# Retention attention feeding a gated FFN on one core: an earlier place for the first weight loads, and the small tables built on other engines

## The chip, the core and the metric

The kernel runs on one core of a Trainium2 chip. A core has a matrix engine (TensorE, PE in the profile), a vector engine (VectorE, DVE), a scalar engine (ScalarE, ACT), GpSimd (POOL), a queue engine (SyncE, SP), and 16 DMA engines that move data between the main memory and the on-chip memory. The engines run side by side and wait for one another through semaphores. Each engine works through its own instructions in order. The metric is device time in microseconds; the time before is a median of 228.19 us over 8 runs.

## What is computed

Two stages follow each other. The first is a retention recurrence over 768 steps for 4 batches and 8 heads of width 64; the second is a feed-forward network with a sigmoid gate on the 3072 resulting rows of width 512 (inner width 1536):

```python
gamma = 1.0 - 2.0 ** (-5.0 - np.arange(H))          # one decay per head
for t in range(S):                                   # S = 768
    state = gamma * state + k[:, :, t] (outer) v[:, :, t]
    y[:, :, t] = scale * q[:, :, t] @ state
x = y.transpose(0, 2, 1, 3).reshape(B * S, H * D)    # 3072 x 512
gate = sigmoid(x @ w_gate); val = x @ w_val          # 512 x 1536 each
out = (gate * val) @ w_out                           # 1536 x 512
```

All inputs and the output are float32 in main memory; the matrix products are in bf16.

## The kernel before

The recurrence is cut into 6 tiles of 128 steps. Within a tile the sum over earlier steps is a masked 128x128 score matrix per head (with powers of gamma as the mask), and what lies in earlier tiles comes through a 64x64 state per head. The feed-forward part of one tile (512 rows: 4 batches of 128 steps) has 12 column groups of the gate and value products (`up_part`, L413) and then the output product (`down`, L449). The order of all instructions is written out by hand: the first tile line by line (L486 to L581), the later tiles by a list of group numbers (`plan`), in which attention of later tiles is put between matmul groups.

What matters here is the first tile, where everything starts at once:

- The first two batches' k come in float32 through SP and ACT (`kf`, L101 and L102) and are cast to bf16 in two halves, one by VectorE (L173), one by ScalarE (L174).
- All other loads of the first tile cast while they move, and are issued by GpSimd: q of batches 0 and 1, k and q of batches 2 and 3, v of batches 0 to 3 (L109 to L117, ten loads). Then come the first weights (`load_w`, L79): `wg` and `wv`, columns 0 to 255, each in two halves of 128 KB (as they land, in bf16), and then columns 256 to 511 and 512 to 767 with 256 KB a load (slabs 1 and 2). GpSimd's loads take turns on eight semaphores, so the ninth and every later load waits until the load eight places before it has landed.
- Tables. `ahead` and `after` (L110, L111) are index tables that GpSimd's iota makes. From `after` VectorE makes four exponents of the mask (`decay_power`, L152), which ScalarE takes through exp (`decay_exp`, L156). `ident` (L147), the identity for the transposes, comes from `ahead`. `lgz` (L146) holds the logarithms of the decays. `tok`, `begin` and `col` (L118 to L120) are three more iotas; from `col` and `lgz` GpSimd makes the exponents of `taby` (L189), from `tok` and `begin` VectorE makes those of `tabs` and `tabz` (`later_constants`), and ScalarE takes these three through exp (`later_exps`, L184 to L186). `taby` is first used by the second tile.
- TensorE: 11 dummy products on zeros (`keep_on`, L480; further ones fill later waits), transposes of k and q (`first_transpose`, L352), scores (L362), which VectorE masks (L369), the product with v (`first_y`, L379), copied into `xT` (L384), and then the first gate and value products (`first_part`, L422), first over k-tiles 0 and 1, then over 2 and 3, so that each half of the weights is used when it lands. After that follow the groups of L413.
- GpSimd's further work behind the slabs: `first_scaled` (L388, two products for each half), which wait for the exp of `tabs`, more weight loads, the tables of the later tiles.

Of the kernel before, what the change touches and what calls it, by code (L numbers as in the profile page):

```python
# [10 lines left out]
AX = mybir.ActivationFunctionType  # L11
ALU = mybir.AluOpType
# [3 lines left out]
def kernel(  # L16
# [12 lines left out]
    nc = tc.nc  # L29
    B, H, S, D = q.shape  # L30
    N_TOK, D_MODEL = out.shape
    D_FF = moe_w_gate.shape[1]
    C = 128
    NT = S // C
    NP = H // 2
# [37 lines left out]
    wg = wpool.tile([128, KT, D_FF], BF16, name="wg")  # L73
    wv = wpool.tile([128, KT, D_FF], BF16, name="wv")
    wo = wpool.tile([128, NFF, D_MODEL], BF16, name="wo")

    def load_w(dst, w, s, kk=slice(0, KT)):
        cols = slice(s * 256, (s + 1) * 256)
        nc.gpsimd.dma_start(out=dst[:, kk, cols], in_=w.rearrange("(kk p) n -> p kk n", p=128)[:, kk, cols])  # L79

    def load_gate_val(s):
        load_w(wg, moe_w_gate, s)
        load_w(wv, moe_w_val, s)
# [8 lines left out]
    def first(dst, x, b, eng):  # L92
        j = b % 2
        eng.dma_start(out=dst[j * D:(j + 1) * D].rearrange("p h r d -> p h (r d)"),  # L94
                      in_=x[b, :, 0:C, :].rearrange("h (p r) d -> p h (r d)", r=2))

    kf = ld.tile([C, H, 2, D], F32, tag="kf", name="kf", bufs=1)
    k2, q2, v2 = [[ld.tile([C, H, 2, D], BF16, tag=tag, name=tag, bufs=n) for _ in range(2)]
                  for tag, n in (("kn", 6), ("qn", 4), ("vs", 6))]
# [4 lines left out]
    ahead = const.tile([128, C], F32, name="ahead")  # L104
    after = const.tile([128, 3, D], F32, name="after")
    tok = const.tile([128, NT], F32, name="tok")
    begin = const.tile([128, NT], F32, name="begin")
    col = const.tile([128, C], F32, name="col")
    first(q2[0], q, 0, nc.gpsimd)  # L109
    nc.gpsimd.iota(ahead, pattern=[[-1, C]], base=0, channel_multiplier=1, allow_small_or_imprecise_dtypes=True)  # L110
    nc.gpsimd.iota(after, pattern=[[1, 3], [-2, D]], base=-1, channel_multiplier=2, allow_small_or_imprecise_dtypes=True)  # L111
    first(q2[0], q, 1, nc.gpsimd)
    for x, t in ((k, k2[1]), (q, q2[1])):
        for b in (2, 3):
            first(t, x, b, nc.gpsimd)
    for b in range(4):
        first(v2[b // 2], v, b, nc.gpsimd)  # L117
    nc.gpsimd.iota(tok, pattern=[[C, NT]], base=0, channel_multiplier=1, allow_small_or_imprecise_dtypes=True)  # L118
    nc.gpsimd.iota(begin, pattern=[[C, NT]], base=0, channel_multiplier=0, allow_small_or_imprecise_dtypes=True)
    nc.gpsimd.iota(col, pattern=[[1, C]], base=0, channel_multiplier=0, allow_small_or_imprecise_dtypes=True)  # L120

# [3 lines left out]
    nlg = const.tile([128, 2, NP], F32, name="nlg")  # L127
    lgz = const.tile([128, 2, NP], F32, name="lgz")
    lsc = const.tile([128, 1], F32, name="lsc")
    ident = const.tile([128, 128], BF16, name="ident")  # L130
# [5 lines left out]
    taby = const.tile([128, NP, C], F32, name="taby")  # L136
# [3 lines left out]
    nc.vector.memset(lsc, math.log(scale))  # L140
    for h in range(H):
        nc.vector.memset(nlg[:, h % 2, h // 2:h // 2 + 1], -lg[h])
    for e in range(2):
        hd = slice(e * D, (e + 1) * D)
        for j in range(2):
            nc.vector.tensor_scalar(lgz[hd, j], nlg[hd, e ^ j], -1.0, None, op0=ALU.mult)  # L146
    nc.vector.tensor_scalar(ident, ahead, 0.0, None, op0=ALU.is_equal)  # L147
    nc.vector.tensor_scalar(after[D:128], after[D:128], -2.0 * D, None, op0=ALU.add)
    since = after.rearrange("s r p -> s (r p)")

    def decay_power(g, e):
        nc.vector.tensor_tensor(decay[:, g, e], since.unsqueeze(1).to_broadcast([128, 2, 3 * D]),  # L152
                                nlg[:, e, 2 * g:2 * g + 2].unsqueeze(2).to_broadcast([128, 2, 3 * D]), op=ALU.mult)

    def decay_exp(g, e):
        nc.scalar.activation(decay[:, g, e], decay[:, g, e], AX.Exp, bias=lsc)  # L156
# [3 lines left out]
    def tab_power(x, lo, n):  # L160
        nc.vector.tensor_tensor(tabs_of[:, :, :, lo:lo + n], x.unsqueeze(1).unsqueeze(1).to_broadcast([128, NP, 2, n]),
                                nlg.rearrange("s e p -> s p e").unsqueeze(3).to_broadcast([128, NP, 2, n]), op=ALU.mult)
# [1 line left out]
    tab_power(after[:, 1:3, 0], NT, 2)  # L164
    nc.vector.scalar_tensor_tensor(since, since, -1.0e6, since, op0=ALU.mult, op1=ALU.min)
    kb = k2[0]
    decay_power(0, 0)
    decay_power(0, 1)
    decay_power(1, 0)
    decay_exp(0, 0)  # L170
    decay_exp(0, 1)
    decay_exp(1, 0)
    nc.vector.tensor_copy(kb[:, 0:4], kf[:, 0:4])  # L173
    nc.scalar.copy(kb[:, 4:8], kf[:, 4:8])  # L174
    decay_power(1, 1)

    def later_constants():
        tab_power(tok, 0, NT)
        shape = [128, NT, 2, NP]
        nc.vector.tensor_tensor(tabz, lgz.unsqueeze(1).to_broadcast(shape),  # L180
                                begin.unsqueeze(2).unsqueeze(3).to_broadcast(shape), op=ALU.mult)

    def later_exps():
        nc.scalar.activation(taby, taby, AX.Exp, bias=lsc)  # L184
        nc.scalar.activation(tabs, tabs, AX.Exp)
        nc.scalar.activation(tabz[:, 1:], tabz[:, 1:], AX.Exp)  # L186

    def taby_power():
        nc.gpsimd.tensor_tensor(taby, col.unsqueeze(1).to_broadcast([128, NP, C]),  # L189
                                lgz[:, 0].unsqueeze(2).to_broadcast([128, NP, C]), op=ALU.mult)  # L190

    taby_power()
    for dst, w in ((wg, moe_w_gate), (wv, moe_w_val)):
        load_w(dst, w, 0, slice(0, 2))
        load_w(dst, w, 0, slice(2, 4))
    load_gate_val(1)
    load_gate_val(2)

    def last_constants():
        nc.vector.tensor_scalar(causal, ahead, 0.0, None, op0=ALU.is_le)  # L200
# [15 lines left out]
    def bank(shape, dt=F32):  # L216
        return pf.tile(shape, dt, tag="ff", name="ff")

    def half(e):
        return slice(e * D, (e + 1) * D)  # L220
# [126 lines left out]
    def first_transpose(i, which, g, eng):  # L347
        tp = bank([128, 2, 2, C], BF16)
        for p in range(2):
            for r in range(2):  # L350
                for e in range(2):
                    nc.tensor.transpose(tp[half(e), p, r ^ which], (k2, q2)[which][i][:, 4 * g + 2 * p + e, r, :], ident)  # L352
        eng(kq2[i][:, which, 2 * g:2 * g + 2], tp)

    def first_scores(i, g):
        t = kq2[i]
        s = [bank([128, 2, 2, C]) for _ in range(2)]
        for p in range(2):
            for r in range(2):
                for j in range(2):  # L360
                    for e in range(2):
                        nc.tensor.matmul(s[e][half(j), p, r].rearrange("s (o p) -> s o p", o=2),  # L362
                                         t[half(e), 0, 2 * g + p, r, half(j)], t[half(e), 1, 2 * g + p, :, half(j)],
                                         start=True, stop=True)
        for e in range(2):
            st0[i, g, e] = at.tile([128, 2, 2, C], BF16, tag=f"st{e}", name=f"st{e}", bufs=4)
            d = decay[:, g, e]
            d = bass.AP(d.tensor, d.offset, [d.ap[0], d.ap[1], (D, 2), (1, C)])
            nc.vector.tensor_tensor(st0[i, g, e], s[e], d, op=ALU.mult)  # L369
# [107 lines left out]
    def keep_on(n):  # L477
        u = bank([128, 512])
        for _ in range(n):
            nc.tensor.matmul(u, zero[:, :128], zero, start=True, stop=True)  # L480
# [5 lines left out]
    keep_on(11)  # L486
    first_transpose(0, 0, 0, dve)
    first_transpose(0, 0, 1, act)
    decay_exp(1, 1)
    keep_on(1)  # L490
    first_transpose(0, 1, 0, dve)
    first_transpose(0, 1, 1, act)
    keep_on(1)
    first_scores(0, 0)
    first_scores(0, 1)
    later_constants()
    keep_on(1)
    first_transpose(1, 0, 0, act)
# [6 lines left out]
    first_y(0, (act, act))  # L505
    first_scores(1, 1)
    later_exps()
    keep_on(3)
    gate0 = first_part(wg, 0)
# [128 lines left out]
```

## Time and profile before

| What | Value |
|---|---|
| median of 8 runs | 228.19 us (227.27 to 230.99) |
| the profiled execution's own time | 230.57 us |
| its span in the profile | 228.8 us |
| TensorE busy | 218.8 us (96%) |
| VectorE / ScalarE / GpSimd busy | 111.3 / 69.9 / 105.9 us |
| bytes moved by DMA | 25.75 MB, mean 113 GB/s |
| granted TensorE clock over the span | 0.991 of full speed |

The profiled execution is one of the eight runs, and one of the longest. 1.77 us of its time lie outside the span. Times in the profile count from the start of the span. An operation's line gives its start, the time that it takes (for a group of several: from the first start to the last end), the engine, the source line, what it writes and reads, and, in brackets, how long the engine sat idle before it and what ended the wait. A DMA has two parts: the short instruction with which a queue issues it, and the transfer, which lands some us later. The GB/s and DMA rows count the bytes that the 16 DMA engines moved and how busy these were.

### The profile page before, as it was taken

Reading aid. Unit: us, or ns where it says so; the run is one execution under the profiler, and the core shown is the slowest. Engines: PE = TensorE matmul, PEld = TensorE weight load, DVE = VectorE, ACT = ScalarE, POOL = GpSimd, SP = SyncE. Lnnn points to the kernel's source line nnn. Section 1 sums busy time; section 2 is a strip of 40 time slices with the busy share of each in tenths; the row PEclk is TensorE's granted clock in tenths of the full one; section 3 lists DMA queues with packets and bytes.
Section 4 is the critical chain, followed back from the end, with each engine's and each line's share of the span. In section 5 each row is a group of like instructions: output and inputs, shape, how many; then the busy total and the mean of one; then the engine's idle time right before and its main releaser. Section 6 shows DMA issues by size and latency. Waiting matters only on the chain.

```text
span 228.8 us, 4913 instructions
## 1 busy us (share of the span) xinstructions
PE 218.8 (96%) x2037; PEld 118.2 (52%) x2061; DVE 111.3 (49%) x193; ACT 69.9 (31%) x117; POOL 105.9 (46%) x133
## 2 busy tenths in 40 slices
PE   7876999999999999999999999999999999999994
PEld 2545444547888655445445444545444444444443
DVE  6751384145784676944914634923544812343301
ACT  4654323432223211433311433211433311433221
POOL 7999697960994986719276073370000000000000
PEclk9997999999999999999999999999999999999999
DMA  7999999998999999999979879799500012100022
GB/s 125 177 146 168 196 146 169 185 146 179 138 131 126 190 154 197 148 106 90 125 93 161 172 52 117 75 133 141 133 6 0 3 46 95 46 1 0 3 92 92
DMA packets 99702, 25.75 MB, mean 113 GB/s; under 512 B 87648, under 2 KB 96736, under 8 KB 99680
## 3 DMA queue, kind: packets, MB, share of 16 engines
q0 software_dynamic: 75808, 13.90, 76.4%
q1 hardware_dynamic: 23200, 11.21, 23.4%
q10 hardware_dynamic: 672, 0.33, 0.5%
q8 instruction: 16, 0.26, 0.5%
q14 instruction: 6, 0.05, 0.1%
HBM read 28.31 MB, written 6.29 MB: 151 GB/s over the span
## 4 chain that ended last, share of the span: by engine, by line
PE 90%; POOL 5%; DMA 3%; issue 1%; DVE 0%; POOLq 0%
PE ff L413 53%; PE ff L449 26%; DMA wv<-in_moe_w_val_dram 3%; PE ff L284 2%; PE ff L261 2%; PE ff L422 2%; PE ff L277 2%; POOL qn L94 1%; PE ff L466 1%; PE ff L302 1%; POOL vs L94 1%; POOL wg L79 1%; POOL kn L94 1%; POOL taby L189 0%; PE ff L232 0%
## 5 line engine op out<-in xcount | busy, mean ns | idle before, releaser
L433 DVE TENSOR_TENSOR hT<-gs,ff 128x512 bf16<-128x512 f32 x72 | 49.0, 686 | 62.6 <-PE ff L413 57.8
L413 PE MATMUL ff<-xT,wg 128*128 128x512 bf16 (+1 forms) x323 | 71.5, 348 | 0.6 <-issue 0.2
L413 PE MATMUL ff<-xT,wv 128*128 128x512 bf16 (+1 forms) x324 | 71.0, 347 | 0.1
L432 ACT ACTIVATE gs<-ff 128x512 f32<-128x512 f32 x72 | 43.0, 597 | 85.6 <-PE ff L413 80.3
L449 PE MATMUL ff<-wo,hT 128*128 128x512 bf16 x263 | 60.9, 379 | 1.0 <-issue 0.5
L413 PEld LDWEIGHTS <-wv 128*128 128x128 bf16 x328 | 32.1, 98 | 28.4
L413 PEld LDWEIGHTS <-wg 128*128 128x128 bf16 x328 | 31.8, 98 | 28.2 <-issue 0.6
L449 PEld LDWEIGHTS <-hT 128*128 128x128 bf16 x276 | 26.3, 98 | 30.7
L453 ACT COPY ob<-ff 128x512 f32<-128x512 f32 x23 | 13.5, 586 | 58.4 <-PE ff L449 56.3
L267 DVE TENSOR_TENSOR st<-ff,maskk 128x512 bf16<-128x512 f32 x40 | 24.8, 682 | 6.4 <-PE ff L261 6.4
L295 DVE TENSOR_TENSOR xT<-ff,taby 128x512 bf16<-128x512 f32 x20 | 12.9, 686 | 30.3 <-PE ff L284 30.3
L548 POOL COPY held<-kqX 128x1 bf16<-128x1 bf16 x7 | 1.3, 184 | 39.9 <-DMA kqX<-qn 32.4
L243 POOL TENSOR_TENSOR ks<-kn,tabsk 128x1024 bf16<-128x1024 bf16 x8 | 16.0, 2001 | 0.5 <-PE ff L413 0.3
L67 POOL DMA_DIRECT2D qn<-in_q_dram x20 | 15.4, 802 | 0.0
L67 POOL DMA_DIRECT2D kn<-in_k_dram x20 | 15.2, 774 | 0.0
L57 POOL DMA_DIRECT2D vs<-in_v_dram x10 | 12.1, 1212 | 0.6 <-DMA kn<-in_k_dram 0.5
L63 POOL DMA_DIRECT2D kn<-in_k_dram x10 | 9.3, 929 | 1.8 <-issue 1.8
L63 POOL DMA_DIRECT2D qn<-in_q_dram x10 | 9.3, 926 | 0.0
L480 PE MATMUL ff<-zero 128*128 128x512 bf16 x19 | 7.6, 528 | 1.2 <-DVE zero L139 1.2
L315 DVE TENSOR_TENSOR zb<-za,tabz 128x512 bf16<-128x512 f32 x10 | 8.5, 857 | 0.2
L284 PE MATMUL ff<-st,vs 128*64 128x128 bf16 x160 | 6.4, 222 | 0.0
L261 PE MATMUL ff<-kqX 64*64 64x128 bf16 x288 | 5.6, 217 | 0.0
(80 smaller groups left out, 117.5 us busy)
## 6 DMA issues: line engine op xcount, KB each, us to landing
out_dram<-ob SPq DMA_DIRECT2D x19, 256.0 KB, 3.0
vs<-in_v_dram POOLq DMA_DIRECT2D x10, 256.0 KB, 7.5
qn<-in_q_dram POOLq DMA_DIRECT2D x14, 128.0 KB, 4.5
kn<-in_k_dram POOLq DMA_DIRECT2D x12, 128.0 KB, 4.3
wo<-in_moe_w_out_dram POOLq DMA_DIRECT2D x4, 384.0 KB, 6.9
wg<-in_moe_w_gate_dram POOLq DMA_DIRECT2D x5, 256.0 KB, 8.4
wv<-in_moe_w_val_dram POOLq DMA_DIRECT2D x5, 256.0 KB, 9.0
kn<-in_k_dram POOLq DMA_DIRECT2D x20, 64.0 KB, 4.4
```

The source lines that it names most:

```text
L57: nc.gpsimd.dma_start(out=vs[i], in_=v[2 * h:2 * h + 2, :, t * C:(t + 1) * C, :].rearrange("b h s d -> s (b h) d"))
L63: nc.gpsimd.dma_start(out=tiles[i][:, 0:H], in_=src[0])
L67: nc.gpsimd.dma_start(out=dst[:, e], in_=pairs[:, 1 - e])
L243: nc.gpsimd.tensor_tensor(ks[i], kn[i], tabsk[:, i // 2].rearrange("s j h -> s (j h)").unsqueeze(2) .to_broadcast([C, 2 * H, D]), op=ALU.mult)
L267: nc.vector.tensor_tensor(st[i, j], sc[i, j][e], maskk[:, e ^ j], op=ALU.mult)
L284: nc.tensor.matmul(y[i, j][half(e), p, :], vs[i][:, j * H + 2 * p + e, :], st[:, p, :], start=False, stop=True, skip_group_check=True)
L295: nc.vector.tensor_tensor(xT[t][:, :, c:c + C], y[i, j], taby, op=ALU.mult)
L413: nc.tensor.matmul(u[:, i * n:(i + 1) * n], w[:, kk, n1 * 128:(n1 + 1) * 128], xT[t][:, kk, lo:hi], start=(kk == 0), stop=(kk == KT - 1))
L432: nc.scalar.activation(g, ps[0], AX.Sigmoid)
L433: nc.vector.tensor_tensor(hT[t][:, n1s[0]:n1s[-1] + 1, lo:hi], g.rearrange("p (i n) -> p i n", n=n), ps[1].rearrange("p (i n) -> p i n", n ...
L449: nc.tensor.matmul(o, hT[t][:, n1, b * C:(b + 1) * C], wo[:, n1, :], start=(n1 == 0), stop=(n1 == NFF - 1))
L453: nc.scalar.copy(ob, o)
```

## The change

The weight loads of columns 0 to 767 are issued right behind the four loads of v. The iotas of `tok`, `begin` and `col` and the product for `taby`, which stood between them on GpSimd, are gone from it: VectorE now makes `begin` by six memsets, `col` from `ahead`, `taby`'s exponents behind `lgz`, and `tok` from `begin` and `ahead`. The iotas of `ahead` and `after` stand ahead of GpSimd's first load (q of batch 0) and not behind it. On VectorE, `ident` and `lgz` come after the four `decay_power`s, all four of which, and `col` and `taby`, stand ahead of its half of the cast of k. On ScalarE the fourth `decay_exp` stands with the other three, ahead of the cast of k, and the exp of `taby` moves from behind the first two copies into `xT` to a place behind the transposes of q of batches 0 and 1. TensorE's order is as it was.

```diff
-    first(q2[0], q, 0, nc.gpsimd)
     nc.gpsimd.iota(ahead, pattern=[[-1, C]], base=0, channel_multiplier=1, allow_small_or_imprecise_dtypes=True)
     nc.gpsimd.iota(after, pattern=[[1, 3], [-2, D]], base=-1, channel_multiplier=2, allow_small_or_imprecise_dtypes=True)
+    first(q2[0], q, 0, nc.gpsimd)
     first(q2[0], q, 1, nc.gpsimd)
...
     for b in range(4):
         first(v2[b // 2], v, b, nc.gpsimd)
-    nc.gpsimd.iota(tok, pattern=[[C, NT]], base=0, channel_multiplier=1, allow_small_or_imprecise_dtypes=True)
-    nc.gpsimd.iota(begin, pattern=[[C, NT]], base=0, channel_multiplier=0, allow_small_or_imprecise_dtypes=True)
-    nc.gpsimd.iota(col, pattern=[[1, C]], base=0, channel_multiplier=0, allow_small_or_imprecise_dtypes=True)
+    for dst, w in ((wg, moe_w_gate), (wv, moe_w_val)):
+        load_w(dst, w, 0, slice(0, 2))
+        load_w(dst, w, 0, slice(2, 4))
+    load_gate_val(1)
+    load_gate_val(2)
...
-    for e in range(2):
-        hd = slice(e * D, (e + 1) * D)
-        for j in range(2):
-            nc.vector.tensor_scalar(lgz[hd, j], nlg[hd, e ^ j], -1.0, None, op0=ALU.mult)
-    nc.vector.tensor_scalar(ident, ahead, 0.0, None, op0=ALU.is_equal)
+    for t in range(NT):
+        nc.vector.memset(begin[:, t:t + 1], float(t * C))
...
-    decay_power(0, 0)
-    decay_power(0, 1)
-    decay_power(1, 0)
-    decay_exp(0, 0)
-    decay_exp(0, 1)
-    decay_exp(1, 0)
+    for g in range(2):
+        for e in range(2):
+            decay_power(g, e)
+            decay_exp(g, e)
+    nc.vector.tensor_scalar(ident, ahead, 0.0, None, op0=ALU.is_equal)
+    for e in range(2):
+        hd = slice(e * D, (e + 1) * D)
+        for j in range(2):
+            nc.vector.tensor_scalar(lgz[hd, j], nlg[hd, e ^ j], -1.0, None, op0=ALU.mult)
+    nc.vector.tensor_scalar(col, ahead, ahead[:, 0:1], -1.0, op0=ALU.subtract, op1=ALU.mult)
+    nc.vector.tensor_tensor(taby, col.unsqueeze(1).to_broadcast([128, NP, C]),
+                            lgz[:, 0].unsqueeze(2).to_broadcast([128, NP, C]), op=ALU.mult)
     nc.vector.tensor_copy(kb[:, 0:4], kf[:, 0:4])
     nc.scalar.copy(kb[:, 4:8], kf[:, 4:8])
-    decay_power(1, 1)

     def later_constants():
+        nc.vector.tensor_scalar(tok, begin, ahead[:, 0:1], None, op0=ALU.add)
...
     def later_exps():
-        nc.scalar.activation(taby, taby, AX.Exp, bias=lsc)
...
-    def taby_power():
-        nc.gpsimd.tensor_tensor(taby, col.unsqueeze(1).to_broadcast([128, NP, C]),
-                                lgz[:, 0].unsqueeze(2).to_broadcast([128, NP, C]), op=ALU.mult)
-
-    taby_power()
-    for dst, w in ((wg, moe_w_gate), (wv, moe_w_val)):
-        load_w(dst, w, 0, slice(0, 2))
-        load_w(dst, w, 0, slice(2, 4))
-    load_gate_val(1)
-    load_gate_val(2)
...
     first_transpose(0, 0, 1, act)
-    decay_exp(1, 1)
     keep_on(1)
     first_transpose(0, 1, 0, dve)
     first_transpose(0, 1, 1, act)
+    nc.scalar.activation(taby, taby, AX.Exp, bias=lsc)
     keep_on(1)
```

## The prediction, made before the result was known

> **What bounds the kernel now.** I read the page's first parts, then the chain of waits in order of time, then each engine's timeline for the first 24 us, then the DMA rows of that stretch.
>
> ```profile
> span 228.8 us, 4913 instructions
> PE 218.8 (96%) x2037; PEld 118.2 (52%) x2061; DVE 111.3 (49%) x193; ACT 69.9 (31%) x117; POOL 105.9 (46%) x133
> PEclk9997999999999999999999999999999999999999
> ```
>
> TensorE is the bound, and once it runs it hardly stops. What a change in the first tile can bring is therefore what TensorE waits there. The clock row shows a 7 in the fourth slice, which is where that waiting ends. The chain in order of time runs through GpSimd and one weight load until 18.86 us, and after that through TensorE to the end with gaps of some 0.05 us:
>
> ```profile
> 8.76 0.18 POOL tok L118
> 8.94 0.10 POOL begin L119
> 9.04 0.21 POOL col L120
> 9.24 0.07 issue
> 9.32 1.04 POOL taby L189
> 10.36 1.44 POOL wg L79 x2
> 11.80 0.70 POOL wv L79
> 12.50 6.31 DMA wv<-in_moe_w_val_dram
> 18.81 0.05 issue
> 18.86 3.62 PE ff L422 x20
> ```
>
> TensorE's timeline has two waits of size:
>
> ```profile
> 12.65 0.82 PE L480 MATMUL ff<-zero 128*128 128x512 bf16 x2
> 14.65 1.08 PE L422 MATMUL ff<-xT,wg 128*128 128x256 bf16 x8 [1.17 <-DMA wg<-in_moe_w_gate_dram]
> 15.66 0.64 PE L379 MATMUL ff<-st,vs 64*64 64x128 bf16 x32
> 16.27 0.61 PE L422 MATMUL ff<-xT,wv 128*128 128x256 bf16 x4
> 18.86 0.61 PE L422 MATMUL ff<-xT,wv 128*128 128x256 bf16 x4 [1.97 <-DMA wv<-in_moe_w_val_dram]
> 20.56 1.91 PE L422 MATMUL ff<-xT,wv 128*128 128x256 bf16 x8
> ```
>
> Together 3.14 us of waiting on weights. Eight products of 128x256 take 1.08 us at 14.65 and 1.91 us at 20.56: from 19.8 to 23.2 us the granted clock is 0.50. These 3.4 us do the work of 1.7, so the dip costs 1.7 us. It follows the stretch from 16.35 to 19.77, in which TensorE worked only 1.45 of 3.4 us.
>
> **The change, part by part.**
>
> *GpSimd ahead of the weights.* The first weight issue moves from 10.36 to 8.76: 1.60 us (0.18 + 0.10 + 0.21 + 0.07 + 1.04). The two iotas ahead of q0 only trade places with its issue (0.81 us), so q1 and all behind it are issued as before; q0 goes out at about 1.85 and not 1.26, but q of batches 0 and 1 are used together, and q1's place stays. Should the 0.62 us of issue ahead of q0 not stand ahead of an iota, all of GpSimd is up to 0.6 us earlier. The semaphores in turn hold nothing: the four halves wait for k2, k3, q2 and q3, landed by 7.6, 8.3, 9.0 and 9.8, and would be issued at 8.8, 9.5, 10.2 and 10.9. `first_scaled` would be reached at about 14.6 (16.19 before) and waits for the exp of `tabs`. That ends at 14.37 now, 0.6 earlier without `taby`'s exp (0.73) in front: no stall. Behind it, the loads of slab 3 come earlier with the rest.
>
> *What the 1.6 us buy.* The transfer rate from 4 to 16 us, in steps of 0.3 us, decides:
>
> ```profile
> GB/s 259 210 190 172 168 172 175 178 178 178 178 172 165 178 176 180 179 176 182 174 182 176 179 178 180 172 161 184 174 113 135 172 159 155 140 130 138 131 106 142
> ```
>
> From 5 to 12.4 us it is flat at 165 to 184. The ten q, k and v loads stand in line at the DMA engines: a load is issued every 0.67 us and one is carried every 0.73 us (128 KB at 178). Their last packets go at 12.34, while the first packets of `wg` go at 11.95. So weights issued at 8.76 stand in the same line and find no free engines before about 12.3. Only the dip to 113 and 135 at 12.7 to 13.3, and part of the slower time after it, is want of issued work. [...]
>
> Worked out: ideal carrying from 12.3 on at 178 ends the four halves at 12.3 + 4 x 0.73 = 15.2 us; in the trace their 512 KB (1024 packets) are carried by 15.8. So 0.6 us is the most that the average engine gains at the second half of `wv`. But a load has landed only when all 16 engines are done. The trace's completion marks of that load lie between 15.4 and 16.9 for 14 engines, and at 18.75 and 18.81 for the last two. Single packets of 0.4 to 1.2 us (60 ns is usual) stand in the stretch from 12.2 to 19.3, among the first weights touched. An engine held by such packets is not short of work: the last marks of the two halves of `wg` are at 14.60 and 15.07, closer together than their issues (0.77 apart). It gains between 0 and 0.4. Bounds for the landing of the second half of `wv`: 0 (the held engines set it) and 1.6 (holds go with the time of issue). I take 0.5, by the flat row and the 0.6.
>
> *The next that is late.* At full clock TensorE takes 2.2 us from 18.86 for the other 20 products of L422, then 1.7 for two gate groups, and asks for slab 1 of `wv` at 22.8. That load was issued at 13.97 and took 9.0 us: it lands at 23.0. So half a microsecond from the first waits arrives only if slab 1 comes as much earlier; its issue does (1.6), its place in line gives the same 0.5 or more.
>
> *VectorE.* Its half of the cast of k waits for data now:
>
> ```profile
> 3.69 1.50 DVE L152 TENSOR_TENSOR decay<-after,nlg 128x384 f32<-128x384 f32 x3
> 5.97 0.43 DVE L173 CAST kn<-kf 128x512 bf16<-128x512 f32 x1 [0.78 <-DMA kf<-in_k_dram]
> ```
>
> After: `after` is ready 0.8 us earlier (1.87 for 2.68), and the chain to the first exponent keeps its 0.9 us, so this starts at 2.81. Four at 0.47 apart end at 4.70; `ident` 0.25 (row 0.30), `lgz` 0.33 (0.49 for four, 0.16 of it tail), `col` 0.25 (as `ident`; 0.2 to 0.4, as no such row has a tile as its scalar), `taby` 0.60 (nearest row: the mask product of 128x512, 1.29 for two; GpSimd's own 1.04 is the upper bound): 6.13, and 0.1 for the wait of `taby` on `col`. The cast starts at 6.2 and not 5.97: 0.2 us later, bounds 0 and 0.7. TensorE's transposes move with it, 6.45 to 6.65, and so does all up to the gate product. Its input is ready at 13.6 and it waited for weights until 14.65: 1.0 us of cover, of which 0.5 is left if `wg` comes earlier. So this costs nothing; with no cover it would cost 0.2. The fourth exponent no longer stands at 6.31, ahead of the first copy of transposes (6.90), which waits for TensorE anyway. `begin` (six memsets, 0.17 for eight now) and `tok` (a 128x6 operation, under 0.2) lie in waits for `after` (0.68) and for scores.
>
> [...] Row: GpSimd's issues beside the cast at 5.97 take 0.72 and 0.73 us, as their neighbours do. [...]
>
> *ScalarE.* The fourth exp leaves 7.61. `taby`'s exp (0.73) comes at about 8.7, in the wait of 1.18 us ahead of the copy at 9.88; copies wait for TensorE, so it is hidden with 0.4 to spare. Behind it, the exp of `tabs` is earlier.
>
> **Sum.** Against the profiled execution: 230.57 - 0.5 = 230.1 with the dip, 228.4 without. The eight runs fall into 227.27 to 228.42 (six) and 230.57 and 230.99: I read the latter two as those with the dip, the profile's among them. Against the median: 228.19 - 0.5 = 227.7, and 0.1 less for a dip that becomes rarer as the wait of 1.97 shrinks: 227.6.
>
> **The rivals.**
>
> *The line at the engines moves with the issue (faster).* If the holds of single packets come from loads that trickle in, both waits go: 3.14 us, less 0.3 for the cast of k that is then on the path: 228.19 - 2.8 = 225.4. With the 1.6 alone it is 226.6. For it: 14 of 16 marks of the `wg` and `wv` halves lie 2.9 to 3.3 us behind the issue, as for loads that found free engines. Against it: the flat row, and the two late engines.
>
> *One longer wait, and a dip in every run (slower).* If the halves of `wg` and the first of `wv` land earlier and the held engine keeps the last half at 18.8, TensorE works off what it has by 15.9 and then idles 2.9 us in one piece. The end of the wait is where it was, and the dip, now in two runs of eight, is in all: 230.6 (mean of the two 230.8, less 0.2). [...] Against it: a gain of 1 us at the first `wg` half needs the held engine to gain it, and then it gains on the last half too.
>
> *It brings nothing*, because slab 1 of `wv` still lands at 23.0: 228.1, inside the likeliest case's range.
>
> **How the numbers follow.** Likeliest, 0.60: 227.6, its own range 226.6 to 228.8. Faster rival 0.25 (225.2 to 226.6), slower rival 0.15 (230.0 to 231.0). Within 1% (2.3 us, about what a measurement of this kernel can tell from no change) lie the likeliest and the upper part of the faster rival: 0.64; faster 0.22, slower 0.14. Range 225.4 to 230.2.
>
> **What would show it.** First weight issue at 8.8 or earlier; the rate flat to 13 us with no dip to 113; the cast of k at 5.9 to 6.4; the gate product at 14.1; second half of `wv` landing at 18.3; slab 1 at 22.5. The forecast is wrong if that half lands by 16.5 (faster), or if the clock is 0.50 beside a wait above 2.5 us (slower), or if VectorE's row reaches past 7 us.

## The result, and the profile after

| | before | changed |
|---|---|---|
| median | 227.78 us (56 runs, 226.97 to 231.43) | 226.63 us (19 runs, 226.03 to 228.02) |
| ratio, 95% interval | | 0.9946 (0.9929 to 0.9963) |
| profiled execution: time, span | 230.57, 228.8 us | 227.06, 225.3 us |

The changed kernel is faster by 0.5% (1.2 us): inside the range, within 1%, and about twice the forecast of 0.6. A second measurement, under the experiments, gives 0.5 us. The profiled execution of before that is shown above was one with a dip of the clock; a second profile of the same kernel, without one, is the fairer partner below.

The page's first lines and clock row of the changed kernel:

```profile
span 225.3 us, 4917 instructions
PE 216.4 (96%) x2037; PEld 117.4 (52%) x2061; DVE 116.1 (52%) x202; ACT 69.9 (31%) x117; POOL 103.8 (46%) x129
PEclk9999999999999999999999999999999999999999
```

The 7 in the clock row is gone. The chain of waits in order of time, around the weights (start, duration, what):

```profile
5.62 2.72 POOL vs L94 x4
8.34 1.35 POOL wg L79 x2
9.69 6.04 DMA wv<-in_moe_w_val_dram
15.72 0.05 issue
15.77 2.91 PE ff L415 x24
18.68 0.05 issue
18.73 1.46 PE ff L406 x6
```

The first weight is issued at 8.3 us (10.36 before), and the load on the chain is now the first half of `wv`, not the second. TensorE's timeline after the change (L415 and L406 are the former L422 and L413):

```profile
12.75 0.82 PE L473 MATMUL ff<-zero 128*128 128x512 bf16 x2
13.76 1.03 PE L415 MATMUL ff<-xT,wg 128*128 128x256 bf16 x8 [0.18 <-ACT xT L377]
14.72 0.64 PE L372 MATMUL ff<-st,vs 64*64 64x128 bf16 x32
15.77 1.16 PE L415 MATMUL ff<-xT,wv 128*128 128x256 bf16 x8 [0.41 <-DMA wv<-in_moe_w_val_dram]
17.64 1.04 PE L415 MATMUL ff<-xT,wv 128*128 128x256 bf16 x8
18.73 1.67 PE L406 MATMUL ff<-xT,wg 128*128 128x512 bf16 x7
```

Of 3.14 us of waiting on weights 0.41 are left, and the first large group starts at 18.73 and not at 22.70 (19.06 in the second profile of before). The transfer rate from 4 to 16 us, in steps of 0.3 us:

```profile
GB/s 236 200 189 175 181 178 177 178 179 176 183 174 183 176 178 181 173 184 173 184 176 181 178 178 178 183 189 192 190 198 188 251 176 184 183 191 195 193 201 186
```

It no longer falls where the weights begin. The 0.41 us that are left end with one DMA engine out of 16: 15 completion marks of the first half of `wv` lie by 14.75, the last one at 15.72. In the DMA rows from 4 to 16 us one packet is no data but instructions:

```profile
q8 instruction: 1, 0.02, 0.5%
```

It is of 16 KB and took 0.98 us from 13.49, where a packet of the loads takes 0.04 or 0.06. That it held the late engine fits in time and length; the trace does not name the engine of a packet, so this is argued and not shown.

What the start gains is not all kept; VectorE at 76 us, and GpSimd beside it:

```profile
75.93 0.68 DVE L304 TENSOR_TENSOR za<-za,ff 128x512 f32<-128x512 f32 x1
76.65 4.24 DVE L308 TENSOR_TENSOR zb<-za,tabz 128x512 bf16<-128x512 f32 x1
80.81 1.28 DVE L288 TENSOR_TENSOR xT<-ff,taby 128x512 bf16<-128x512 f32 x2
```

```profile
75.33 1.21 POOL L57 DMA_DIRECT2D vs<-in_v_dram  x1
76.50 3.83 POOL L236 TENSOR_TENSOR ks<-kn,tabsk 128x1024 bf16<-128x1024 bf16 x2
```

A product that takes 0.69 us in the median of its ten places took 4.24 and ended 0.56 us after GpSimd's two products. TensorE then waited 0.77 us for the `xT` behind it (at 81.5). In the profile of before the same two met with VectorE first by 0.04 us, and its product took 0.69:

```profile
80.86 0.69 DVE L315 TENSOR_TENSOR zb<-za,tabz 128x512 bf16<-128x512 f32 x1
80.90 4.28 POOL L243 TENSOR_TENSOR ks<-kn,tabsk 128x1024 bf16<-128x1024 bf16 x2
```

### The profile page after: what moved, and what is told of

It reads as the page before. It is cut to its first block, busy times and chain, and to the rows that moved or that the text cites. A ratio compares the mean times of both kernels' runs of the same rounds, so it can differ in the third digit from the quotient of the medians.

```text
span 225.3 us, 4917 instructions
## 1 busy us (share of the span) xinstructions
PE 216.4 (96%) x2037; PEld 117.4 (52%) x2061; DVE 116.1 (52%) x202; ACT 69.9 (31%) x117; POOL 103.8 (46%) x129
## 3 DMA queue, kind: packets, MB, share of 16 engines
q1 hardware_dynamic: 23200, 11.21, 22.6%
## 4 chain that ended last, share of the span: by engine, by line
PE 87%; DVE 4%; POOL 4%; DMA 3%; issue 1%; POOLq 0%; DVEq 0%
PE ff L406 54%; PE ff L442 24%; DMA wv<-in_moe_w_val_dram 3%; PE ff L277 2%; DVE zb L308 2%; PE ff L254 2%; PE ff L270 1%; PE ff L415 1%; POOL qn L94 1%; POOL vs L94 1%; PE ff L459 1%; DVE st L260 1%; PE ff L295 1%; POOL kn L94 1%; POOL wg L79 1%
## 5 line engine op out<-in xcount | busy, mean ns | idle before, releaser
L406 PE MATMUL ff<-xT,wg 128*128 128x512 bf16 (+1 forms) x323 | 71.3, 348 | 0.4
L406 PE MATMUL ff<-xT,wv 128*128 128x512 bf16 (+1 forms) x324 | 71.0, 347 | 0.1
L406 PEld LDWEIGHTS <-wv 128*128 128x128 bf16 x328 | 32.1, 98 | 28.5
L406 PEld LDWEIGHTS <-wg 128*128 128x128 bf16 x328 | 31.6, 98 | 27.9
L236 POOL TENSOR_TENSOR ks<-kn,tabsk 128x1024 bf16<-128x1024 bf16 x8 | 15.5, 1955 | 0.8 <-DMA kn<-in_k_dram 0.8
L308 DVE TENSOR_TENSOR zb<-za,tabz 128x512 bf16<-128x512 f32 x10 | 11.8, 1190 | 0.2
L473 PE MATMUL ff<-zero 128*128 128x512 bf16 x19 | 6.8, 480 | 1.2 <-DVE zero L141 1.2
```

Of the source, the lines that this page charges most:

```text
L236: nc.gpsimd.tensor_tensor(ks[i], kn[i], tabsk[:, i // 2].rearrange("s j h -> s (j h)").unsqueeze(2) .to_broadcast([C, 2 * H, D]), op=ALU.mult)
L308: nc.vector.tensor_tensor(zb[i], za[i], tabz[:, i // 2 + 1].unsqueeze(3).to_broadcast([128, 2, NP, D]), op=ALU.mult)
L406: nc.tensor.matmul(u[:, i * n:(i + 1) * n], w[:, kk, n1 * 128:(n1 + 1) * 128], xT[t][:, kk, lo:hi], start=(kk == 0), stop=(kk == KT - 1))
```

## The experiments

"Slow packets" below are data packets of the loads that took above 0.15 us (0.04 or 0.06 is usual), counted in the trace between 11 and 20 us. The profile of before has 52, the one of the changed kernel none. The count says nothing of later loads: every profile has some slow packets between 24 and 36 us, the changed kernel 12 of 0.15 to 0.23 us from 28.2 to 30.0.

**A second profile of before.** No edit.

> The kernel before, unchanged, for a second profile of it. Theory 'line and holds' (weights trickle in behind v, and some DMA engines are held by single packets of 0.4 to 1.2 us in every execution of this order): slow packets are there again between 12 and 19 us, the last half of wv lands at 17.5 to 19, TensorE waits 1.5 to 3 us in sum on weights. Rival 'the holds are chance': no packets above 0.2 us beside the instruction fetch, the last half of wv lands at issue + 3.5 = 16.0, TensorE waits under 1.2 us in sum, span about 226.0.

46 slow packets, 227.24 us. The last half of `wv` landed at 16.45 and not at 18.81, TensorE waited 0.62 us on weights before L422 and 0.21 before L413:

```profile
14.33 1.08 PE L422 MATMUL ff<-xT,wg 128*128 128x256 bf16 x8 [0.62 <-DMA wg<-in_moe_w_gate_dram]
19.06 1.90 PE L413 MATMUL ff<-xT,wg 128*128 128x512 bf16 x8 [0.21 <-DMA wg<-in_moe_w_gate_dram]
```

So the holds are there in both profiles of before, but what they cost varies: 2.4 us between the two profiles at that load, and then the dip on top. Each theory had half: the packets of the first, the landing of the second.

**The changed kernel again.** No edit.

> The changed kernel, unchanged, for a second profile and a time beside the kernels of this call. Theory 'no holds where the weights follow v without a gap': at most three packets above 0.15 us between 12 and 19 us, last half of wv at 15.2 to 16.3, first group of L406 at 18.6 to 19.0, time 0.4 to 0.7% below the kernel before. Rival 'the holds are chance in both': more than 20 slow packets again, L406 from 19.5 on.

No slow packets again, last half of `wv` at 16.41 (0.1 later than expected), L406 at 18.65. The time was 0.9979 of before (0.9958 to 1.0001; 227.26 against 227.72): less than the 0.4% expected, and not quite clear of no change, so the gain of the change is better told as 0.2 to 0.5%. The undisturbed profiles agree with the small end: 19.06 to 18.73 or 18.65 at the first group, 0.3 to 0.4 us. `zb` took 2.58 us at most here, and TensorE's wait behind it was not there.

**The weights late, all else changed.**

```diff
+    pad = const.tile([128, C], F32, name="pad")
+    padw = const.tile([128, NP, C], F32, name="padw")
+    nc.gpsimd.iota(pad[:, 0:NT], pattern=[[C, NT]], base=0, channel_multiplier=1, allow_small_or_imprecise_dtypes=True)
+    nc.gpsimd.iota(pad[:, NT:2 * NT], pattern=[[C, NT]], base=0, channel_multiplier=0, allow_small_or_imprecise_dtypes=True)
+    nc.gpsimd.iota(pad, pattern=[[1, C]], base=0, channel_multiplier=0, allow_small_or_imprecise_dtypes=True)
+    nc.gpsimd.tensor_tensor(padw, pad.unsqueeze(1).to_broadcast([128, NP, C]),
+                            pad[:, 0:NP].unsqueeze(2).to_broadcast([128, NP, C]), op=ALU.mult)
     for dst, w in ((wg, moe_w_gate), (wv, moe_w_val)):
         load_w(dst, w, 0, slice(0, 2))
```

> The changed kernel with the three small iotas and a 128x512 product put back on GpSimd between the loads of v and the weights (into tiles that nothing reads), all tables still made on VectorE and ScalarE. Theory 'the place of the weight loads is all of the gain': first weight issue at about 9.9 (8.3 in the changed kernel), time at 227.5 to 227.9, as the kernel before. Rival 'the tables and the iotas ahead bring it, as the DMA engines are backlogged': 226.4 to 226.9, as the changed kernel.

227.49 us, 0.9976 (0.9959 to 0.9992), first issue at 10.0. The median lies at the edge of the first expectation, but its ratio is still below 1, which that theory did not have, and the time does not tell it from the changed kernel's second measurement. So the time does not show how much of the gain is the place of the weights. The trace shows what the place does: 48 slow packets are back with the late issue, L413 starts at 19.02, and TensorE waits for `wg`:

```profile
14.47 1.11 PE L422 MATMUL ff<-xT,wg 128*128 128x256 bf16 x8 [0.94 <-DMA wg<-in_moe_w_gate_dram]
```

This wait also ends with one engine (15 marks by 13.23, the last at 14.43), behind an instruction packet of 0.97 us at 12.19. The rate from 4 to 16 us:

```profile
GB/s 228 194 177 183 163 168 173 171 175 170 177 178 177 180 178 178 178 179 178 178 178 180 177 180 173 165 131 235 178 176 195 106 116 120 111 174 173 111 116 121
```

**Half of that delay.**

```diff
+    padw = const.tile([128, NP, C], F32, name="padw")
+    nc.gpsimd.tensor_tensor(padw, ahead.unsqueeze(1).to_broadcast([128, NP, C]),
+                            ahead[:, 0:NP].unsqueeze(2).to_broadcast([128, NP, C]), op=ALU.mult)
     for dst, w in ((wg, moe_w_gate), (wv, moe_w_val)):
```

> The changed kernel with only a 128x512 product on GpSimd between v and the weights: first weight issue at about 9.3, between the changed kernel (8.3, no slow packets) and the one with the full delay (10.0, 53 slow packets). Theory 'the line at the DMA engines must not run dry' (first packets of the weights come 1.5 us behind the issue, v's last packets at 12.3): a lead of 3.0 us is enough, under 10 slow packets. Rival 'it grows with the lateness': 20 to 35.

First issue at 9.23, 8 slow packets, the longest 0.35 us; L409 (the former L413) at 18.68; 226.85 us in one run. TensorE still waits 0.72 us for `wg`, whose last mark (14.21, the others by 13.32) again follows an instruction packet, at 11.94. The lead of the first weight issue over v's last packet is 4.1 us in the changed kernel (none slow), 3.1 here (8), 2.2 with the full delay (48) and 2.0 and 2.1 before (52 and 46).

**v late together with the weights.**

```diff
+    pad = const.tile([128, C], F32, name="pad")
...
+    nc.gpsimd.tensor_tensor(padw, pad.unsqueeze(1).to_broadcast([128, NP, C]),
+                            pad[:, 0:NP].unsqueeze(2).to_broadcast([128, NP, C]), op=ALU.mult)
     for b in range(4):
         first(v2[b // 2], v, b, nc.gpsimd)
     for dst, w in ((wg, moe_w_gate), (wv, moe_w_val)):
```

> The changed kernel with the three iotas and the product on GpSimd ahead of the loads of v and not behind them: the weights follow v without a gap, both 1.6 us later, first weight issue at about 9.9. Theory 'a gap between v and the weights makes the holds': under 10 slow packets, slab 0 of wv lands by 16.6. Rival 'it is how far the issue runs ahead of the line': the line is 1.6 us shorter, 30 to 60 slow packets among the weights, slab 0 of wv at 16.4 to 18.8.

The lines left out are those of the full delay. 34 slow packets, eight of them v's own (from 11.2 us on): the third and fourth load of v landed at 13.01 and 13.92, where the same kernel without the delay has 11.98 and 12.82. No gap lies between v and the weights here, and the first weight issue leads v's last packet by 3.35 us, more than the 3.1 of half the delay. The short lead is v's: its first load is issued 1.7 us before all bytes ahead of it are carried (3.4 in the changed kernel), and the slow packets begin among v's loads. So neither the gap nor the weights as such make the holds; in these runs they begin where a load is issued with little work left in the line at the DMA engines (1.7 us here). 228.41 us in one run; TensorE's wait:

```profile
15.32 1.25 PE L422 MATMUL ff<-xT,wg 128*128 128x256 bf16 x8 [1.74 <-DMA wg<-in_moe_w_gate_dram]
```

**Whole slabs in the order of before.**

```diff
-        load_w(dst, w, 0, slice(0, 2))
-        load_w(dst, w, 0, slice(2, 4))
+        load_w(dst, w, 0)
```

> The kernel before with the first slab of wg and of wv loaded by one issue each (256 KB) and not by two, so that from the second weight issue on the line at the DMA engines does not run dry; first issue still at 10.3. Theory 'an engine that runs out of issued work is held': under 15 slow packets between 12 and 19 us, slab 0 of wv lands by 15.9, TensorE waits for slab 0 of wg until about 14.3. Rival 'the late first issue as such brings the holds': 40 to 60 slow packets as before, slab 0 of wv at 16.4 to 18.8.

33 slow packets, between the two expectations; the landing was the rival's. `wg` landed at 15.26 and `wv` at 16.60, L412 (the former L413) started at 19.49, 227.61 us. More bytes behind the first late issue did not remove the holds.

**The weights moved alone.**

```diff
     for b in range(4):
         first(v2[b // 2], v, b, nc.gpsimd)
+    for dst, w in ((wg, moe_w_gate), (wv, moe_w_val)):
+        load_w(dst, w, 0, slice(0, 2))
+        load_w(dst, w, 0, slice(2, 4))
+    load_gate_val(1)
+    load_gate_val(2)
     nc.gpsimd.iota(tok, pattern=[[C, NT]], base=0, channel_multiplier=1, allow_small_or_imprecise_dtypes=True)
     nc.gpsimd.iota(begin, pattern=[[C, NT]], base=0, channel_multiplier=0, allow_small_or_imprecise_dtypes=True)
     nc.gpsimd.iota(col, pattern=[[1, C]], base=0, channel_multiplier=0, allow_small_or_imprecise_dtypes=True)
...
     taby_power()
-    for dst, w in ((wg, moe_w_gate), (wv, moe_w_val)):
-        load_w(dst, w, 0, slice(0, 2))
-        load_w(dst, w, 0, slice(2, 4))
-    load_gate_val(1)
-    load_gate_val(2)
```

> The kernel before with one part of the change alone: the first ten weight issues' worth of loads (slabs 0 to 2) stand right behind v, and the three small iotas and the product for taby stay on GpSimd, behind them. Theory 'the tables had to move off GpSimd': the iotas come at about 14.7, VectorE's tabs and tabz wait for them with the second pair's four masks queued behind (12.1 before, 15.2 now), the product with v of the second pair starts at 17.0 and not 15.7, L413 at 20.8 to 21.5 (19.06 in the second profile of before), time 229.3 to 230.5. Rival 'the place of the weight loads is all of the gain': 226.7 to 227.2.

230.21 us, 1.0072 (1.0036 to 1.0108): slower than before, as the first theory had it. VectorE's timeline shows why:

```profile
14.83 0.21 DVE L166 TENSOR_TENSOR tabs<-tok,nlg 128x48 f32<-128x48 f32 x1 [3.46 <-POOL tok L123]
14.96 0.20 DVE L185 TENSOR_TENSOR tabz<-lgz,begin 128x48 f32<-128x48 f32 x1
15.08 2.48 DVE L369 TENSOR_TENSOR st<-ff,decay 128x512 bf16<-128x512 f32 x4
```

Two operations of 0.2 us wait 3.46 us for an iota that now lies behind eight loads, and four masks wait behind them. The product with v was done at 18.2, the clock fell to 0.50 from 16.5 to 19.9, and L413 started at 21.85. Eight of the ten runs show a mean granted clock of 0.993 or less. The line was well fed here until the eighth load, and no packet was slow up to 20 us; the next load was issued at 19.2, when the line had nearly run out, and 17 slow packets came at 20.85 to 22.6. They follow the short line, not the time since the start and not the first rows of a weight.

**q0 ahead of the iotas again.**

```diff
+    first(q2[0], q, 0, nc.gpsimd)
     nc.gpsimd.iota(ahead, pattern=[[-1, C]], base=0, channel_multiplier=1, allow_small_or_imprecise_dtypes=True)
     nc.gpsimd.iota(after, pattern=[[1, 3], [-2, D]], base=-1, channel_multiplier=2, allow_small_or_imprecise_dtypes=True)
-    first(q2[0], q, 0, nc.gpsimd)
     first(q2[0], q, 1, nc.gpsimd)
```

> The changed kernel with the load of q of batch 0 issued ahead of the two iotas again, as before. GpSimd reaches the first weight issue 0.45 us later (8.75), and VectorE's chain starts 0.8 us later, so its half of the cast of k starts at about 6.9. Theory 'hidden': the transposes have cover only up to the gate product (13.76, its wait is 0.2 us on ScalarE's copy), so 0.6 to 0.8 us of the later cast reaches the path: 227.2 to 227.5. Rival 'TensorE's dummies and later waits take it up': within 0.2 us of the changed kernel.

228.67 us, 1.003 (1.0011 to 1.0049): this one line takes back more than the whole change brings. In its profile VectorE's cast of k is at 7.39 (6.16), and TensorE waits for it longer:

```profile
7.87 0.64 PE L345 MATMUL ff<-ident,kn 128*64 128x128 bf16 x16 [1.80 <-DVE kn L178]
```

The gate product moves from 13.76 to 14.97, all of the 1.2 us, but L406 only to 19.14, as the wait for `wv` takes up the rest. That profile took 227.41 us, though, and 18 of the 20 runs took 228.19 or more. The clock of each run tells what this profile does not have: 14 of the 20 have a mean granted clock of 0.991 or 0.992 over the span, as the profile of before with its dip (0.991), and the profiled run has 0.998. The other four long ones (229.28 to 229.44) have 1.000 and stay unexplained.

**The same, with the wait filled.**

```diff
-    keep_on(11)
+    keep_on(15)
```

> The kernel with the load of q0 ahead of the iotas again, and 15 dummy products at the start where there were 11, so that TensorE's wait of 1.80 us for the cast of k is filled to about 1.0 us. Theory 'the clock': this wait makes the clock dip to one half in most executions, which is why its median lay 1.3 us above its profiled execution's: now 227.0 to 227.4. Rival 'the later cast costs all of it on the path': 228.4 to 228.8 as without the dummies.

227.37 us, 0.9976 (0.9955 to 0.9996), no run above 227.9. The cast and all behind it are as late as before (gate product at 14.97, L406 at 19.14); only four dummy products stand in TensorE's wait, which is now 1.27 us:

```profile
7.87 0.64 PE L345 MATMUL ff<-ident,kn 128*64 128x128 bf16 x16 [1.27 <-DVE kn L178]
```

So the 1.3 us came from TensorE idling, not from the late tables. The clocks go with it: none of these 20 runs is below 0.997, where 14 of 20 had a dip without the four products. Where in the run that dip lay was not seen, as no profile caught one.

**`zb` behind the next masks, without and with two more dummies.**

```diff
-            (5, casts, 3), (7, xbar, 5), (7, scale_k, 5), (11, block, None, 4, 4), (12, casts, 4), (12, xbar, 6), (12, scale_k, 6),
-            (12, hold, 6), (12, load_next, 7), (14, block, 4, 5, 5), (16, casts, 5), (18, block, 5, 6, 6), (19, casts, 6)],
+            (5, casts, 3), (7, xbar, 5), (7, scale_k, 5), (11, block, None, 4, 4), (12, xbar, 6), (12, scale_k, 6),
+            (12, hold, 6), (12, load_next, 7), (14, block, 4, 5, 5), (14, casts, 4), (16, casts, 5), (18, block, 5, 6, 6), (19, casts, 6)],
```

> The changed kernel with one product of VectorE moved: zb of the third pair of blocks, at 76.65 us, where it took 4.24 us beside GpSimd's two products of ks, comes behind the next block's masks. [...] Rival 'an artefact of the one profiled execution': no change of time (within 0.2 us).

226.38 us, 0.9933 (0.9914 to 0.9952). The two `zb`s now lie together and are free of GpSimd's products:

```profile
79.42 1.29 DVE L288 TENSOR_TENSOR xT<-ff,taby 128x512 bf16<-128x512 f32 x2 [2.33 <-PE ff L277]
83.61 1.29 DVE L308 TENSOR_TENSOR zb<-za,tabz 128x512 bf16<-128x512 f32 x2
```

TensorE's wait is gone. The start is that of the changed kernel, yet L406 began only at 18.99: the instruction packet came earlier (13.09), the second half of `wg` had its last mark 1.4 us after the 15th, and TensorE waited 0.93 us for it. So the gain at the first group is 0.1 to 0.4 us, by the execution. The time is only 0.1 point below the changed kernel's first ratio, with intervals that overlap. The second profile of the changed kernel has no such wait either, so those 0.77 us belong to some executions and not to all.

> The changed kernel with zb of the third pair of blocks moved behind the next block's masks and 13 dummy products at the start where there were 11. Theory 'the clock' (the wait of 1.2 to 1.4 us for the cast of k costs a dip in some executions): 225.6 to 226.0, with fewer executions above 226.5. Rival 'no dips are left in the changed kernel': 226.2 to 226.5, as with the moved zb alone, or 0.1 to 0.3 more where the cold clock lets the dummies run past the cast.

With `keep_on(13)` added: 226.7 us, 0.9954 (0.9934 to 0.9975). The rival was right: filling the changed kernel's own wait for the cast of k (1.37 us in one profile, 0.59 in the other) with two dummies won nothing that shows. Both versions beat before; neither is told apart from the changed kernel.

## Why the prediction came out as it did

**Right in kind.** The gain is small because the DMA engines had a line of q, k and v until 12.3 us before the change and until 12.4 after it. In the undisturbed pair of profiles the middle one of the 16 completion marks of the last half of `wv` went from 15.8 to 14.9 or 15.1 and the last one from 16.45 to 16.3 or 16.4, with 2.2 us of earlier issue. The chain alone would have promised all of it. The last mark gained less than the middle one because one engine is behind: in the seven profiles without slow packets up to 20 us the last mark of this load comes 0.7 to 1.1 us after the 15th, in the second profile of before 0.06. In each of the seven the first weight load that ends so is the one whose marks come around the end of the instruction packet (0.94 to 0.98 us long, begun at 12.98 to 13.95), and the weight loads before it have their last two marks within 0.1 us. That this packet, and not the line, sets what is left is likely by this, but no run moved it on its own. The faster rival (225.4) asked for both waits to vanish from the median; they vanished from a bad execution only.

**The term that was mis-sized** is the landing of the last half of `wv`: 0.5 us, argued from "an engine held by such packets is not short of work", 0 to 0.4 for that engine. Against the profile the sum was made with, it came 2.5 us earlier (18.81 to 16.27), against the second one 0.2. I took the holds for something fixed to the first rows of the weights that are touched. The runs show them bound to a line with little issued work ahead: none up to 20 us in seven profiles with a lead of 3.6 us or more, 33 to 52 in four with 2.6 or less and in the one with v late, and some at slab 3 where that was issued late. So the change does not only move the weights by the share of the line; it also keeps the slow packets from the first weights. What that is worth in the median is not shown: the whole change brought 1.2 us in one measurement and 0.5 in the other. Fewer dips do not explain it as far as the clocks are on record: in the later measurements 3 of 123 runs of before have a mean clock below 0.995, and of the changed kernel 1 of 40.

**In part by luck.** The last half of `wv` landed at 16.27, and the forecast had named a landing by 16.5 as a sign of the faster rival; the time did not follow. The sign was taken from an execution out of the ordinary, as the second profile of before lands at 16.45 already. The sum took 0.5 us off the median for a term measured on that execution, so that the time fell near the forecast speaks little for the term. Slab 1 of `wv`, called the next that is late, landed at 18.91 and not at 22.5 (20.86 in the second profile of before) and was not waited for. A reading behind the faster rival was wrong too, that 14 of 16 marks of these loads lie 2.9 to 3.3 us behind the issue: the 14th lies 3.1 us behind it for the first half of `wg`, 3.4 for the next two loads and 4.4 for the last half of `wv`. And the first packets of `wg` go at 11.81, not 11.95, which changes nothing.

**GpSimd.** First issue forecast at 8.76, or 0.6 earlier should the 0.62 us not stand ahead of an iota: it did not (iota at 0.84), and the issue was at 8.3. No semaphore held a load.

**VectorE.** The cast of k was forecast at 6.2 and was at 6.16, by another sum: `after` came at 1.3 and the exponents began at 2.25, `lgz` took 0.68 and not 0.33, and the cast still waited 0.19 us for its data. "1.0 us of cover up to the gate product" was wrong: with the weights early there is none there (0.18 us, on ScalarE), as the run with q0 ahead shows. I did not price what the longer wait for k does to the median, which was the dearest thing in the neighbourhood: 1.3 us by a pair of runs.

**ScalarE.** `taby`'s exp at 8.70, in its wait, free: right.

**The slower rival** (one longer wait and a dip in every run) did not come: the held engine lost its slow packets with the rest, and the clock was 1.0. That such a wait brings a dip in all runs, which its 230.6 rests on, was an estimate of mine, and no run shows it. A dip behind a half-empty stretch does occur, as the run of the weights alone shows (0.50 from 16.5 to 19.9). How little work brings one is not settled: it came after 1.45 us of work in 3.4 us before the change and after 1.93 in 3.4 with the weights alone, and the run with v late has a stretch of 3.4 us (from 12.56) with 1.57 and no dip.

**VectorE beside GpSimd.** The sum has no term for the loads' issues beside VectorE's work: right (two issues in 1.35 to 1.48 us). It has none for GpSimd's products either. `zb` at 76.65 took 4.24 us for 0.69, beside two of these, and ended 0.56 us after them; what held it is not shown. The change touches nothing there; it only moved TensorE and GpSimd by different amounts, and where VectorE's product had started 0.04 us ahead it now started 0.15 us behind. The run with v late has it too (4.30 us, GpSimd first by 0.09). Near a tie the start times do not tell which it will be: in the second profile of the changed kernel such a product starts 0.03 us ahead of GpSimd's, at 90.78, and takes 2.58 us. That gave a gain back in one of the two profiles of the changed kernel (0.77 us of TensorE's waiting), and I had no term for it.

## What to carry to other kernels

How early a load was issued mattered less here than whether the line at the DMA engines stayed fed (no slow packet up to 20 us with a lead of 3.6 us or more, 33 to 52 with 2.6 or less): look how far issues run ahead of the packets, not only at issue to landing of one load. Before a load is moved forward, look which small tables fall behind it and who is queued behind their first reader; with the weights moved alone, that made this change a loss (1.0072 of before). And when a median lies away from its profile by more than the profiles differ, look at the granted clock of every run, and for waits of TensorE that only some executions pay for.

## What was not expected of the hardware

- Between 11 and 20 us, packets of 0.15 to 1.8 us appear when the first weight issue leads v's last packet by some 2 us, and not at a lead of 3.6 us or more: 52, 46, 48 against 0 in seven profiles. Why single packets are slow then stays open.
- The order of one 0.8 us load and two iotas at the start was worth 0.5 to 0.8% of the whole kernel, by the wait that it makes TensorE idle for; 14 of 20 runs then have a clock of 0.991 or 0.992.
- A product on VectorE that starts within 0.15 us of two on GpSimd took 0.69 or 4.24 us, and the start times do not always tell which it will be.
- Where no packet of data is slow, the last of 16 marks of a load can still come 1 us behind the other 15 (14.75 and 15.72), next to an instruction packet of 0.98 us.
